# A fused attention and maxout kernel: columns of h by chunks of two batches, one store for a tile of 128 rows

## The chip, the cores and the metric

The kernel runs on one core of one Trainium2 chip. The core has a matrix engine (TensorE, PE in the profile, with its weight loads as PEld), a vector engine (VectorE, DVE), a scalar engine (ScalarE, ACT), GpSimd (POOL) and a synchronising engine (SyncE, SP). SP, ScalarE and GpSimd can issue transfers, which 16 DMA engines carry out. The metric is the device time in microseconds of one execution. Unless it says otherwise, a time inside an execution counts from the start of the profiled span.

## The reference, cut to what matters

Attention over 8 batches, 12 heads, 448 positions and 64 dimensions a head; its output, 3584 rows of 768, goes through three weight matrices, an elementwise maximum of the three products, and a fourth matrix.

```python
scores = scale * np.matmul(q, k.transpose(0, 1, 3, 2))
m = np.max(scores, axis=-1, keepdims=True)
e = np.exp(scores - m)
attn = e / (np.sum(e, axis=-1, keepdims=True) + np.exp(-m) + 1e-09)
attn_out = np.matmul(attn, v)                                # (8, 12, 448, 64)
x = attn_out.transpose(0, 2, 1, 3).reshape(B * S, H * D)     # (3584, 768)
h = np.maximum(np.maximum(x @ w1, x @ w2), x @ w3)
out = h @ w_out                                              # (3584, 768), float32
```

## The kernel before

**Tiles.** Everything is kept transposed: xT and hT have the 768 columns on the partitions (6 blocks of 128) and the positions along the free axis. A position s of a batch is split as s = 7p + j, with p from 0 to 63 and j from 0 to 6; the kernel's column for it is j * 64 + p, so a batch has 7 chunks (j) of 64 columns. Two batches share one hT tile of 6 x 896 columns, 448 of the first batch and then 448 of the second. The last product takes 128 columns of hT at a time as its stationary operand and gives an output tile of 128 rows by 768 columns; a pair of batches has 7 such tiles (t = 0 to 6). Rows 0 to 63 of a tile are one chunk and rows 64 to 127 the next, which at t = 3 belong to different batches. As the rows of a chunk lie 7 rows apart in the output, `store` (L582) sends each tile in two transfers of 64 rows.

**Order.** Attention runs by groups of four heads and feeds the products ("pieces") of finished batches into TensorE's free time, by a planner with costs (`book`, `first_free`, `step`). Pairs 0 and 1 (batches 0 to 3) are wholly done that way: `up_piece` (L507) makes h, `out_piece` (L554) makes the output. For batches 4 and 5 `up_piece` makes only a part of the blocks of h. The rest of pair 2 (batches 4 and 5) and all of pair 3 (batches 6 and 7) is done after the attention by `late_pair` (L1052), with Strassen-like products of 2 x 2 blocks: seven products in place of eight. Their order is written out by hand at the end (L1278 to L1314).

- `up_unit(i, f)` makes 2 x 128 rows of x @ w_i for both batches. `product` (L1035) accumulates three matmuls in a PSUM bank; `copy` (L1106) lets ScalarE evict a product that another one needs; `put` (L1091) evicts a sum into h (i = 0) or into the tile c, by VectorE with an addition (L1097) or by ScalarE alone (L1095). `largest` (L1104) takes the maximum of h and c over all columns. In the last pair the third weight's maxima are taken piece by piece (L1100, L1139).
- `h_sum` (L1083) makes the sums of blocks of h that the last product needs; a block is 3 x 384 columns.
- `out_unit(m)` makes the output tiles t = m (named o1) and t = 3 + m (o2) in column halves of 384 (`put`, L1157). VectorE adds two terms (L1168). The half of o1 that needs no second term goes through ScalarE (L1162), but through VectorE (L1164) where `late` holds, which is so in the last pair for m = 1 and 2.
- `last_tile` makes t = 6 by a plain product (L1232), evicted by VectorE (L1212) into o_last.

**Stores.** In pairs 0 to 2 both transfers of a tile are issued by SP. In the last pair the tile's column halves are sent as they come (except o2 for m = 1 and 2, which go whole); the first 64 rows are issued by SP and the other 64 by GpSimd, or by ScalarE for m = 2 and for o_last. A queue issues in order: an issue that waits for its data holds those behind it. The transfers of SP and ScalarE take eight completion semaphores in turn, and an issue waits until the transfer that had its semaphore before has landed.

Of the kernel before, what the change touches and what calls it, by code (L numbers as in the profile page):

```python
# [12 lines left out]
AF = mybir.ActivationFunctionType  # L13
ALU = mybir.AluOpType
ts = bass.ts

MMDT = FP16
LAMBDA = 256.0
# [4 lines left out]
def kernel(  # L23
# [11 lines left out]
    nc = tc.nc  # L35

    B, H, S, D = q.shape
# [66 lines left out]
    def half(n):  # L104
        return slice(n * KC, n * KC + KC)
# [394 lines left out]
    hT = {}  # L500
    outs = {}

    def new_h(b, fc, i):
        if b // 2 not in hT:
            hT[b // 2] = ht_pool.tile([128, NFC, 2 * S], MMDT, tag="hT", name="hT")

    def up_piece(b, fc, i, bank=None, done=False):  # L507
        if not done:
            new_h(b, fc, i)
        dst = hT[b // 2][:, fc, (b % 2) * S : (b % 2) * S + S]  # L510
        p_i = single("p_i") if bank is None else bank
        for dc in range(0 if done else NDC):
            nc.tensor.matmul(
                out=p_i[:, 0:S],
                lhsT=w_sb[i][:, dc, ts(fc, 128)],
                rhs=xT[b][:, dc, :],
                start=(dc == 0),
                stop=(dc == NDC - 1),
            )
        if i == 0 and done and first_free(2.8, 2.25) == "act":  # L520
            nc.scalar.activation(out=dst, in_=p_i[:, 0:S], func=AF.Copy)
        elif i == 0:
            nc.vector.tensor_copy(out=dst, in_=p_i[:, 0:S])
        else:
            book("dve", 2.8, steps[0] + 2)
            nc.vector.tensor_tensor(out=dst, in0=dst, in1=p_i[:, 0:S], op=ALU.max)  # L526

    def up_part(b, fp, i, part, bank=None):
        if fp == 0 and i == 0 and part == 0:
# [49 lines left out]
        if nh == NH - 1:  # L579
            store(2 * bp, t, o_sb, slice(0, DM))  # L580

    def store(b0, t, src, cols, engines=(nc.sync, nc.sync)):  # L582
        for n in range(2):
            b, j = divmod(2 * t + n, NJ)
            rows = out[(b0 + b) * S : (b0 + b + 1) * S].rearrange("(p j) m -> j p m", j=NJ)
            engines[n].dma_start(out=rows[j][:, cols], in_=src[half(n)])  # L586

    pieces = []

# [35 lines left out]
            run_job()  # L625

    NI = len(groups)
    PE_TR = 8

    load_weight(0, 0, 256)  # L630
# [265 lines left out]

    LATE = B - 4
    BESIDE = (0, 1)  # L900
    SOONER = 1

# [149 lines left out]
    def late_pair(p):  # L1052
# [32 lines left out]
        def up_unit(i, f):  # L1085
            w, t = w_sb[i], comb[i]
            u = {}
            c0 = slice(f * 128, f * 128 + 128)
            c1 = slice(DFF // 2 + f * 128, DFF // 2 + f * 128 + 128)

            def put(b, side, bank, other=None):  # L1091
                dst = hp if i == 0 else u["c"]
                dst = dst[:, f + 3 * side if i == 0 else side, b * S : b * S + S]
                if other is None:
                    nc.scalar.activation(out=dst, in_=bank, func=AF.Copy)  # L1095
                else:
                    nc.vector.tensor_tensor(out=dst, in0=other, in1=bank, op=ALU.add)  # L1097
                if i == 2 and ending:
                    h = hp[:, f + 3 * side, b * S : b * S + S]
                    nc.vector.tensor_tensor(out=h, in0=h, in1=dst, op=ALU.max)  # L1100

            def largest():
                dst = hp[:, f:NFC:3]
                nc.vector.tensor_tensor(out=dst, in0=dst, in1=u["c"], op=ALU.max)  # L1104

            def copy(name, bank):  # L1106
                u[name] = part(name, S)
                nc.scalar.activation(out=u[name], in_=bank, func=AF.Copy)

            def p1():  # L1110
                bank_of(u, "a")
                copy("p1", product(u, "a", lambda k: w[:, k, c0], lambda k: x1[:, k], S, True))

            def p2():
                bank_of(u, "s")
                bank = product(u, "s", lambda k: w[:, 3 + k, c0], lambda k: x1[:, 3 + k], S, True)
                if i > 0:
                    u["c"] = tail.tile([128, 2, 2 * S], MMDT, tag="c", name="c", bufs=3)
                put(0, 0, bank, u["p1"])

            def p6():
                copy("u2", product(u, "a", lambda k: t[:, 1, k, c0], lambda k: sx[p, 1][:, k], S, False))

            def p7():
                copy("p7", product(u, "s", lambda k: t[:, 2, k, c0], lambda k: sx[p, 2][:, k], S, True))

            def p5():
                bank = product(u, "a", lambda k: t[:, 0, k, c0], lambda k: sx[p, 0][:, k], S, False)
                put(1, 1, bank, u["p7"])

            def p4():
                bank = product(u, "s", lambda k: t[:, 3, k, c0], lambda k: x2[:, 3 + k], S, False)
                put(1, 0, bank, u["u2"])

            def p3():
                bank = product(u, "a", lambda k: w[:, 3 + k, c1], lambda k: sx[p, 3][:, k], S, False)
                if i == 2 and ending:
                    dst = hp[:, f + 3, 0:S]
                    nc.vector.tensor_tensor(out=dst, in0=dst, in1=bank, op=ALU.max)  # L1139
                else:  # L1140
                    put(0, 1, bank)

            if i == 0:
                return [p1, p2, p7, p6, p5, p4, p3]
            return [p1, p2, p6, p7, p5, p4, p3, largest]

        def out_unit(m):
            t = comb[3]
            u = {}
            r0 = slice(m * 128, m * 128 + 128)  # L1150
            r1 = slice(NT3 + m * 128, NT3 + m * 128 + 128)

            def copy(name, bank):
                u[name] = part(name, S)[:, 0:NW]
                nc.scalar.activation(out=u[name], in_=bank, func=AF.Copy, scale=1.0 / LAMBDA)

            def put(o, nh, bank, other=None, late=m == 2 and ending):  # L1157

                engines = nc.sync, nc.scalar if late else nc.gpsimd
                dst = u[o][:, ts(nh, NW)]  # L1160
                if other is None and not late:
                    nc.scalar.activation(out=dst, in_=bank, func=AF.Copy, scale=1.0 / LAMBDA)  # L1162
                elif other is None:
                    nc.vector.tensor_scalar(  # L1164
                        out=dst, in0=bank, scalar1=1.0 / LAMBDA, scalar2=None, op0=ALU.mult
                    )
                else:
                    nc.vector.scalar_tensor_tensor(  # L1168
                        out=dst, in0=bank, scalar=1.0 / LAMBDA, in1=other, op0=ALU.mult, op1=ALU.add
                    )  # L1170
                t = {"o1": m, "o2": 3 + m}[o]
                if ending and (o == "o1" or m == 0):
                    store(b0, t, dst, ts(nh, NW), engines)
                elif nh == (1 if o == "o1" else 0):
                    store(b0, t, u[o], slice(0, DM), engines if ending else (nc.sync, nc.sync))

            def p1():
                bank_of(u, "a")
                copy("p1", product(u, "a", lambda k: hp[:, k, r0], lambda k: wout_sb[:, k, 0:NW], NW, True))

            def p2():
                bank_of(u, "s")
                u["o1"] = tail.tile([128, DM], FP32, tag="o1", name="o1", bufs=5)
                bank = product(u, "s", lambda k: hp[:, 3 + k, r0], lambda k: wout_sb[:, 3 + k, 0:NW], NW, True)
                put("o1", 0, bank, u["p1"], False)

            def p6():
                copy("u2", product(u, "a", lambda k: sh[1][:, k, r0], lambda k: t[:, 1, k], NW, False))

            def p7():  # L1190
                copy("p7", product(u, "s", lambda k: sh[2][:, k, r0], lambda k: t[:, 2, k], NW, True))

            def p5():
                u["o2"] = tail.tile([128, DM], FP32, tag="o2", name="o2", bufs=3)
                put("o2", 1, product(u, "a", lambda k: sh[0][:, k, r0], lambda k: t[:, 0, k], NW, False), u["p7"])

            def p4():
                put("o2", 0, product(u, "s", lambda k: hp[:, 3 + k, r1], lambda k: t[:, 3, k], NW, False), u["u2"])

            def p3():  # L1200
                bank = product(u, "a", lambda k: sh[3][:, k, r0], lambda k: wout_sb[:, 3 + k, NW:DM], NW, False)
                put("o1", 1, bank, late=ending and m > 0)

            return [p1, p2, p6, p7, p5, p4, p3]

        def last_tile():
# [3 lines left out]
            def columns(c0, c1, cuts, end=None):  # L1210
                def done(bank):
# [5 lines left out]
                        op0=ALU.mult,  # L1217
                    )
                    if end is not None:
                        store(b0, NT - 1, o_last[:, end], end, (nc.sync, nc.scalar if ending else nc.sync))  # L1220

                return plain(hp, NT - 1, c0, c1, cuts, done)

# [121 lines left out]
```

## Time and profile before

| | |
|---|---|
| median of 3 timed runs | 317.21 us (316.23 to 318.7) |
| the profiled execution | 315.63 us, its span 313.9 us |
| TensorE busy | 300.7 us, 96% |
| VectorE busy | 247.7 us, 79% |
| ScalarE busy | 230.7 us, 73% |
| GpSimd busy | 83.0 us, 26% |
| TensorE clock granted | 0.999 |
| bytes written to HBM | 11.01 MB |

The span runs from the program's first instruction to its last; the profiled execution's own time is longer than its span by what lies around it. Busy shares are means over stages with different limits: the attention fills the span up to about 235 us, the late pairs the rest. The profile's views used below are the page (engines, slices, chain), busy time by stretches (with the DMA engines' share and GB/s in its last columns), timelines of one engine or queue, groups of instructions by line and form (count, busy us, mean ns of one, idle time before them), and the list of transfers issued in a stretch (size, median us from issue to landing). In a timeline the columns are start, duration, engine, line, operation, out<-in, form and count; SPq and ACTq are the issuing queues of SP and ScalarE.

### The profile page before, as it was taken

To read this page: it belongs to the slowest core of one execution; us is meant where nothing else is said; L and a number is where in the kernel's file an instruction comes from. 1 tells how busy PE (TensorE), PEld (TensorE's weight loads), DVE (VectorE), ACT (ScalarE), POOL (GpSimd) and SP (SyncE) were. 2 spreads that over 40 slices of the span, in tenths; PEclk is the share of its full clock that TensorE was granted. 3 is DMA by queue.
4 is the path that set the end of the run, shared out by engine and by line. 5 is a ranking of instruction groups with operands and counts; after the bars stand their busy time and mean duration, and the time that the engine had idled before them with its cause. 6 is when DMAs were issued, how large, how long until landed. Compare 5 with 4: busy or idle time off the path is not lost.

```text
span 313.9 us, 11772 instructions
## 1 busy us (share of the span) xinstructions
PE 300.7 (96%) x5132; PEld 213.2 (68%) x5132; DVE 247.7 (79%) x456; ACT 230.7 (73%) x315; POOL 83.0 (26%) x137
## 2 busy tenths in 40 slices
PE   7779999999999999999999999999999999999992
PEld 5557777658999778777666767777765555556551
DVE  3667598999889788888887898877857994989753
ACT  1999859987888988889888899999845457451540
POOL 8644441220434333434332434010000000000220
PEclk9999999999999999999999999999999999999999
DMA  8999999699778999889999999950004000002687
GB/s 152 196 203 205 208 207 203 102 158 176 95 118 138 188 210 143 99 127 180 204 150 145 100 194 217 143 90 2 4 2 102 1 2 0 0 2 70 179 241 215
DMA packets 59348, 40.58 MB, mean 129 GB/s; under 512 B 32256, under 2 KB 56288, under 8 KB 59296
## 3 DMA queue, kind: packets, MB, share of 16 engines
q0 software_dynamic: 25104, 21.80, 47.8%
q1 hardware_dynamic: 33648, 17.21, 26.6%
q8 instruction: 40, 0.66, 0.8%
q10 hardware_dynamic: 544, 0.82, 0.8%
q14 instruction: 12, 0.10, 0.1%
HBM read 42.47 MB, written 11.01 MB: 170 GB/s over the span
## 4 chain that ended last, share of the span: by engine, by line
PE 85%; ACT 6%; DVE 3%; issue 2%; DMA 1%; DVEq 0%; ACTq 0%
PE piece L786 35%; PE bank_a L1038 11%; PE stp L297 9%; PE bank_s L1038 8%; PE av L345 8%; PE p_i L537 4%; ACT eTp L419 3%; PE bank_a L1240 2%; PE piece L537 2%; ACT eT L321 2%; PE den L345 2%; DMA first_k<-in_k_dram 1%; PE piece L560 1%; DVE eS L331 1%; PE num L345 1%
## 5 line engine op out<-in xcount | busy, mean ns | idle before, releaser
L321 ACT ACTIVATE eT<-stp 128x896 f16<-128x896 f32 x147 | 128.9, 920 | 20.5 <-PE stp L297 20.4
L786 PE MATMUL piece<-xT,w 64*64 64x448 f16 x1968 | 120.6, 349 | 0.4 <-DVE xT L400 0.3
L786 PEld LDWEIGHTS <-w 64*64 64x64 f16 x1968 | 76.8, 107 | 18.1 <-issue 1.1
L331 DVE TENSOR_TENSOR eS<-eS,eT 128x896 f16<-128x896 f16 x105 | 64.9, 618 | 3.4 <-ACT eT L321 0.2
L297 PE MATMUL stp<-qkT 64*64 64x448 f16 (+2 forms) x756 | 63.4, 334 | 3.0 <-issue 0.9
L526 DVE TENSOR_TENSOR hT<-hT,piece 128x448 f16<-128x448 f16 x52 | 32.2, 619 | 13.1 <-PE piece L786 8.1
L297 PEld LDWEIGHTS <-qkT 64*64 64x64 f16 x756 | 28.6, 105 | 17.4 <-issue 6.8
L345 PE MATMUL av<-eT,ld_v 64*64 64x448 f16 x588 | 32.2, 349 | 0.0
L400 DVE TENSOR_TENSOR xT<-av,rb 128x448 f16<-128x448 f32 x42 | 24.2, 618 | 8.3 <-PE av L345 6.9
L345 PEld LDWEIGHTS <-ld_v 64*64 64x64 f16 x756 | 26.1, 107 | 6.5 <-issue 0.5
L114 POOL DMA_DIRECT2D ld_v<-in_v_dram x28 | 16.8, 600 | 51.5 <-PE stp L297 31.7
L786 PE MATMUL piece<-w,hT 64*64 64x384 f16 x456 | 29.3, 323 | 0.1
L586 POOL DMA_DIRECT2D out_dram<-o x7 | 3.8, 538 | 93.7 <-DVE o L1168 92.1
L114 POOL DMA_DIRECT2D ld_k<-in_k_dram x26 | 15.4, 596 | 39.1 <-PE stp L297 34.7
L365 ACT ACTIVATE rb<-den 128x896 f32<-128x896 f32 x21 | 19.3, 917 | 8.2 <-PE den L345 8.1
L419 ACT ACTIVATE eTp<-stp 128x768 f16<-128x768 f32 (+3 forms) x24 | 18.1, 821 | 6.0 <-PE stp L297 5.9
L537 PEld LDWEIGHTS <-w 128*128 128x128 f16 x216 | 18.7, 98 | 5.0 <-issue 3.5
L1038 PEld LDWEIGHTS <-comb 128*128 128x128 f16 x132 | 12.9, 98 | 12.2 <-issue 0.4
L786 PEld LDWEIGHTS <-hT 64*64 64x64 f16 x456 | 18.5, 107 | 3.7 <-issue 0.3
L372 ACT ACTIVATE rb<-rb 128x896 f32<-128x896 f32 x21 | 20.0, 952 | 0.2
L537 PE MATMUL p_i<-xT,w 128*128 128x192 f16 (+1 forms) x156 | 16.5, 257 | 0.0
L114 POOL DMA_DIRECT2D ld_q<-in_q_dram x26 | 15.7, 616 | 1.1 <-issue 1.1
(103 smaller groups left out, 404.9 us busy)
## 6 DMA issues: line engine op xcount, KB each, us to landing
out_dram<-o_sb SPq DMA_DIRECT2D x28, 192.0 KB, 4.6
ld_v<-in_v_dram POOLq DMA_DIRECT2D x28, 112.0 KB, 4.1
ld_k<-in_k_dram POOLq DMA_DIRECT2D x26, 112.0 KB, 3.0
ld_q<-in_q_dram POOLq DMA_DIRECT2D x26, 112.0 KB, 4.0
out_dram<-o SPq DMA_DIRECT2D x14, 192.0 KB, 3.1
ld_q<-in_q_dram POOLq DMA_DIRECT2D x11, 224.0 KB, 9.2
ld_k<-in_k_dram POOLq DMA_DIRECT2D x10, 224.0 KB, 9.3
ld_v<-in_v_dram POOLq DMA_DIRECT2D x10, 224.0 KB, 8.5
```

The costliest lines, as they stand in the source:

```text
L114: return eng.dma_start(out=dst[half(hp)].rearrange("p s j d -> p s (j d)"), in_=rows_of(name, i)[half(hp)])
L297: mm = nc.tensor.matmul(out=out[half(c), r], lhsT=qkT[half(r), 0, j, h], rhs=qkT[half(r), 1, q0:q1, h], start=True, stop=True,)
L321: nc.scalar.activation(out=st["eT"][:, j], in_=stp[:, :, 0:S], func=AF.Exp, scale=scale, bias=-math.log(EDIV))
L331: nc.vector.tensor_tensor(out=st["eS"], in0=st["eT"][:, 0] if j == 1 else st["eS"], in1=st["eT"][:, j], op=ALU.add,)
L345: nc.tensor.matmul(out=outs[r][half(c)], lhsT=weights(r, c), rhs=moving(r, c), start=start, stop=stop,)
L372: nc.scalar.activation(out=st["rb"], in_=st["rb"], func=AF.Exp, bias=math.log(LAMBDA), scale=-1.0)
L400: nc.vector.tensor_tensor(out=xT[b][:, 2 * g + r, :], in0=banks[r][:, 0:S], in1=state[i]["rb"][:, r], op=ALU.mult)
L419: nc.scalar.activation(out=eT[:, j0 : j0 + n].rearrange("p j r q -> p r j q"), in_=stp[:, :, 0 : n * nq].rearrange("p r (j q) -> p r j q", ...
L526: nc.vector.tensor_tensor(out=dst, in0=dst, in1=p_i[:, 0:S], op=ALU.max)
L537: nc.tensor.matmul(out=p_i[:, ts(j, nq)], lhsT=w_sb[i][:, dc, ts(2 * fp + j, 128)], rhs=xT[b][:, dc, q0 * KC : q1 * KC], start=(dc == 0), ...
L786: nc.tensor.matmul(out=p["bank"][half(c), 0:w], lhsT=lhs(k, r, c), rhs=rhs(k, r), start=(r == p["first"] and k == 0), stop=(r != p["first" ...
L1038: nc.tensor.matmul(out=bank, lhsT=lhs(k), rhs=rhs(k), start=start and k == 0, stop=k == 2, skip_group_check=True,)
```

## The change

For batches 4 to 7 the columns of h (and of the tile c) are ordered by chunk first and by batch second: column j * 128 + n * 64 + p for batch n of the pair. So an eviction of one batch's 448 columns writes 7 runs of 64 columns, 128 apart (`h_columns`), and reads its bank in the same shape (`by_chunk`). An output tile then holds chunk t of both batches; with 448 = 64 * 7 its 128 rows lie 7 rows apart throughout, across the batches' border, and one transfer stores them.

The stores of the last pair are all issued by SP, except the second column half of t = 2, which ScalarE issues. The second output of m = 2 (t = 5) is sent in two column halves. The second column halves of t = 1 and t = 2 of the last pair are evicted by ScalarE in place of VectorE. The tile o_last stays with VectorE.

Against the program before, the order of the computing instructions on each engine is the same but for those two evictions; VectorE has two instructions fewer and ScalarE two more. ScalarE's instructions in the late pairs gain 19 waits for VectorE, and TensorE one wait for an earlier matmul of its own.

```diff
+    def h_columns(t, b):
+        if b < LATE:
+            return t[:, (b % 2) * S : (b % 2) * S + S].rearrange("p (j q) -> p j q", j=NJ)
+        return t.rearrange("p (j n q) -> p n j q", j=NJ, n=2)[:, b % 2]
+
+    def by_chunk(t):
+        return t.rearrange("p (j q) -> p j q", j=NJ)
...
-        dst = hT[b // 2][:, fc, (b % 2) * S : (b % 2) * S + S]
+        dst = h_columns(hT[b // 2][:, fc], b)
...
-    def store(b0, t, src, cols, engines=(nc.sync, nc.sync)):
+    def store(b0, t, src, cols, engine=nc.sync):
+        if b0 >= LATE:
+            rows = out[b0 * S : (b0 + 2) * S].rearrange("(p j) m -> j p m", j=NJ)
+            engine.dma_start(out=rows[t][:, cols], in_=src)
+            return
         for n in range(2):
             b, j = divmod(2 * t + n, NJ)
             rows = out[(b0 + b) * S : (b0 + b + 1) * S].rearrange("(p j) m -> j p m", j=NJ)
-            engines[n].dma_start(out=rows[j][:, cols], in_=src[half(n)])
+            engine.dma_start(out=rows[j][:, cols], in_=src[half(n)])
...
             def put(b, side, bank, other=None):
-                dst = hp if i == 0 else u["c"]
-                dst = dst[:, f + 3 * side if i == 0 else side, b * S : b * S + S]
+                dst = h_columns((hp if i == 0 else u["c"])[:, f + 3 * side if i == 0 else side], b0 + b)
                 if other is None:
-                    nc.scalar.activation(out=dst, in_=bank, func=AF.Copy)
+                    nc.scalar.activation(out=dst, in_=by_chunk(bank), func=AF.Copy)
                 else:
-                    nc.vector.tensor_tensor(out=dst, in0=other, in1=bank, op=ALU.add)
+                    nc.vector.tensor_tensor(out=dst, in0=by_chunk(other), in1=by_chunk(bank), op=ALU.add)
                 if i == 2 and ending:
-                    h = hp[:, f + 3 * side, b * S : b * S + S]
+                    h = h_columns(hp[:, f + 3 * side], b0 + b)
                     nc.vector.tensor_tensor(out=h, in0=h, in1=dst, op=ALU.max)
...
-            def put(o, nh, bank, other=None, late=m == 2 and ending):
-
-                engines = nc.sync, nc.scalar if late else nc.gpsimd
+            def put(o, nh, bank, other=None):
                 dst = u[o][:, ts(nh, NW)]
-                if other is None and not late:
+                if other is None:
                     nc.scalar.activation(out=dst, in_=bank, func=AF.Copy, scale=1.0 / LAMBDA)
-                elif other is None:
-                    nc.vector.tensor_scalar(
-                        out=dst, in0=bank, scalar1=1.0 / LAMBDA, scalar2=None, op0=ALU.mult
-                    )
                 else:
...
-                if ending and (o == "o1" or m == 0):
-                    store(b0, t, dst, ts(nh, NW), engines)
+                if ending and (o == "o1" or m != 1):
+                    store(b0, t, dst, ts(nh, NW), nc.scalar if t == 2 and nh == 1 else nc.sync)
                 elif nh == (1 if o == "o1" else 0):
-                    store(b0, t, u[o], slice(0, DM), engines if ending else (nc.sync, nc.sync))
+                    store(b0, t, u[o], slice(0, DM))
...
-                        store(b0, NT - 1, o_last[:, end], end, (nc.sync, nc.scalar if ending else nc.sync))
+                        store(b0, NT - 1, o_last[:, end], end)
```

More of the change, by code (lines that the diff above doesn't have):

```diff
@@ L520, in up_piece @@
         if i == 0 and done and first_free(2.8, 2.25) == "act":
-            nc.scalar.activation(out=dst, in_=p_i[:, 0:S], func=AF.Copy)
+            nc.scalar.activation(out=dst, in_=by_chunk(p_i[:, 0:S]), func=AF.Copy)
         elif i == 0:
-            nc.vector.tensor_copy(out=dst, in_=p_i[:, 0:S])
+            nc.vector.tensor_copy(out=dst, in_=by_chunk(p_i[:, 0:S]))
         else:
             book("dve", 2.8, steps[0] + 2)
-            nc.vector.tensor_tensor(out=dst, in0=dst, in1=p_i[:, 0:S], op=ALU.max)
+            nc.vector.tensor_tensor(out=dst, in0=dst, in1=by_chunk(p_i[:, 0:S]), op=ALU.max)
     def up_part(b, fp, i, part, bank=None):
@@ L627 @@
     NI = len(groups)
+    LATE = B - 4
     PE_TR = 8
@@ L894 @@
     TOTAL = sum(w for _, _, w in ORDER)
-    LATE = B - 4
     BESIDE = (0, 1)
@@ L1137, in p3 @@
                 if i == 2 and ending:
-                    dst = hp[:, f + 3, 0:S]
-                    nc.vector.tensor_tensor(out=dst, in0=dst, in1=bank, op=ALU.max)
+                    dst = h_columns(hp[:, f + 3], b0)
+                    nc.vector.tensor_tensor(out=dst, in0=dst, in1=by_chunk(bank), op=ALU.max)
                 else:
@@ L1184, in p2 @@
                 bank = product(u, "s", lambda k: hp[:, 3 + k, r0], lambda k: wout_sb[:, 3 + k, 0:NW], NW, True)
-                put("o1", 0, bank, u["p1"], False)
+                put("o1", 0, bank, u["p1"])
             def p6():
@@ L1201, in p3 @@
                 bank = product(u, "a", lambda k: sh[3][:, k, r0], lambda k: wout_sb[:, 3 + k, NW:DM], NW, False)
-                put("o1", 1, bank, late=ending and m > 0)
+                put("o1", 1, bank)
             return [p1, p2, p6, p7, p5, p4, p3]
```

## The prediction

> **What bounds the kernel now.** I read the page first (engines, DMA slices), then the last 30 us by stretches, then the timelines of SP's queue and of VectorE, and last the DMA issues with their time to landing.
>
> ```profile
> span 313.9 us, 11772 instructions
> ...
> PE 300.7 (96%) x5132; PEld 213.2 (68%) x5132; DVE 247.7 (79%) x456; ACT 230.7 (73%) x315; POOL 83.0 (26%) x137
> ...
> DMA  8999999699778999889999999950004000002687
> ...
> PE 85%; ACT 6%; DVE 3%; issue 2%; DMA 1%; DVEq 0%; ACTq 0%
> ```
>
> TensorE is busy 96% of the span and makes 85% of the chain. So almost nothing the change does off TensorE can show before the last matmul. But the DMA digits end in 2687: in the last tenth of the span the engines that move data fill up again, and the chain of the page stops at the last computing instruction, so what the stores cost behind it is not in it. That is where I look.
>
> ```profile
> core 0: us, PE busy (x) PEld busy (x) DVE busy (x) ACT busy (x) POOL busy (x), PEclk, DMA share, GB/s
> ...
> 288.10:288.90 0.80, 0.80 (x8) 0.54 (x7) 0.38 (x1) 0.49 (x1) 0.00 (x0) 1.00 0.99 211
> 289.00:289.30 0.30, 0.30 (x7) 0.30 (x5) 0.30 (x1) 0.00 (x0) 0.00 (x0) 1.00 0.85 328
> 302.50:304.50 2.00, 2.00 (x14) 1.21 (x13) 1.11 (x2) 1.21 (x3) 0.08 (x1) 1.00 0.93 238
> ...
> 306.50:308.50 2.00, 1.65 (x17) 1.22 (x14) 1.98 (x5) 0.00 (x0) 0.00 (x0) 1.00 0.90 260
> 308.50:310.50 2.00, 0.00 (x0) 0.00 (x0) 0.05 (x1) 0.00 (x0) 0.00 (x0) 1.00 0.91 267
> 310.50:312.00 1.50, 0.00 (x0) 0.00 (x0) 0.00 (x0) 0.00 (x0) 0.00 (x0) 1.00 0.92 304
> ```
>
> The last column is GB/s, the one before it the busy share of the 16 DMA engines. From 302.5 us to 312.0 us that share never falls under 0.90, so the stores are a queue of their own by then, though they move only 238 to 304 GB/s. The first row holds one transfer of 64 rows alone: busy 0.99 and yet 211 GB/s. In the second the next half has joined, some engines have run ahead, and 328 GB/s pass. All arithmetic ends near 308.5 us, and 5.3 us of the span follow.
>
> ```profile
> 306.98 0.84 SPq L586 DMA_DIRECT2D out_dram<-o_last  x1
> 307.91 1.58 SPq L586 DMA_DIRECT2D out_dram<-o  x2
> 309.68 0.80 SPq L586 DMA_DIRECT2D out_dram<-o_last  x1
> ```
>
> ```profile
> 307.69 0.56 DVE L1164 TENSOR_SCALAR o<-bank_a 128x384 f32<-128x384 f32 x1
> 308.19 0.36 DVE L1212 TENSOR_SCALAR o_last<-bank_a 128x192 f32<-128x192 f32 x1
> ```
>
> ```profile
> out_dram<-o_last SPq DMA_DIRECT2D x1, 96.0 KB, 3.1
> ```
>
> The last eviction ends at 308.19 + 0.36 = 308.55 us. SP issues its store only at 309.68: two earlier issues stand before it, and it then waits for the semaphore that ScalarE's store of o_last (issued 306.32) frees by landing at 309.62. It lands 3.1 us later, at 312.75, and the closing instructions take 1.1 us to 313.86.
>
> **The change, part by part.** The profiled execution took 315.63 us, span 313.86 and 1.77 around it, 1.6 us under the median of 317.21 of the three timed runs. I make the sum in the span and take it off the median.
>
> *1. One transfer of 128 rows in place of two of 64 (batches 4 to 7).* In the stretch of the output tiles, from 286.9 us, SP issues 26 stores, POOL 7 and ScalarE 5, 38 in all for 14 tiles of 384 KB. After it SP issues 19 and ScalarE 1, with the same bytes; tile 5 now goes in two column halves. POOL's 7 issues were on no chain and give nothing. The price of a 128-row transfer is not in this trace. For its time to land, the nearest rows are these:
>
> ```profile
> out_dram<-o SPq DMA_DIRECT2D x2, 192.0 KB, 2.7
> ```
>
> ```profile
> out_dram<-o SPq DMA_DIRECT2D x1, 96.0 KB, 2.2
> ```
>
> Both met idle DMA engines (issued 286.94 and 295.41). The last store of the changed kernel is 192 KB in 128 rows: not under 2.2 us, and not over 2.7 if no backlog is left. I take 2.4, since at 328 GB/s its 197 kB move in 0.6 us and not in the 0.9 of the 211 GB/s row.
>
> Is the backlog gone by then? From 302.5 to 308.5 us the stores now move about 2 x (238 + 290 + 260) = 1.58 MB (the middle stretch moved 290). At 328 GB/s the same 6 us hold 1.97 MB, 0.39 MB more. After 308.5 us 267 x 2 + 304 x 1.5 = 0.99 MB are still moved, of which 0.39 MB are the two pieces that are evicted last. So of 0.60 MB of backlog 0.2 MB are left by this price, 0.6 us of traffic, most of it gone before the last store's first packet (1.1 us behind its issue in the 286.94 one). I add 0.2 us. Ends: 0 and 0.6.
>
> [...]
>
> *2. SP's queue.* With one transfer for two, the issues ahead of the last store are those of o_last's first half (ready at 306.29), and of tile 5's two halves (306.95 and 307.42). An issue takes SP 0.47 us with nothing behind it (rows from 286.94 on, 64 rows, whatever their width). So SP stands free at about 308.0, and issues the last store at 308.57 instead of 309.68. The semaphore that it then waits for belongs to the eighth DMA before it, the store of tile 1's second half, which was evicted at 302.43 and has long landed. Bounds for an issue of 128 rows: 0.47, and twice that, 0.94, where SP is late (a rival below). I take 0.5, the row of one DMA instruction of the same kind.
>
> *3. Evictions moved to ScalarE.* The words of the change say "last tile"; in the diff it is the second column half of tiles 1 and 2 of the last pair that move from VectorE (two of L1164, 0.55 us) to ScalarE (L1162, 0.49). The tile called o_last stays on VectorE. ScalarE is 0.5 us and less busy in each of the last stretches, and loses five DMA issues of about 0.5 us; its store of tile 2 stands behind its own eviction, at the end of its queue. The last eviction waits for TensorE, whose last matmul ends at 308.15, not for VectorE: gain 0 to 0.05 us, I take 0. If ScalarE were late, only tile 2's store would be: 0.5 us of slack towards the last one.
>
> *4. Columns of h by chunks.* All evictions of h and c for batches 4 to 7 write 7 runs of 64 instead of 448 in a row; matmuls read the same 128 columns in a row. Nearest rows:
>
> ```profile
> L214 DVE COPY qk<-ld_k 128x896 f16<-128x896 f16 x16 | 6.4, 402 | 0.0
> ...
> L257 DVE COPY qkT<-trT 128x896 f16<-128x896 f16 x8 | 4.6, 614 | 0.0
> L239 DVE COPY qkT<-trT 128x896 f16<-128x896 f16 x6 | 3.6, 620 | 0.9 <-PE trT L223 0.9
> L1100 DVE TENSOR_TENSOR hT<-hT,c 128x448 f16<-128x448 f16 x9 | 3.5, 392 | 0.3
> ```
>
> L257 writes runs of 64 from PSUM in 614 ns, L239 the same size in one run in 620; L214 works in runs of 64 on both sides at 402 ns for 896. So runs of 64 cost nothing on a copy. A two-operand instruction in SBUF with such runs (L1100) is not shown: between 392 ns and the 618 of the PSUM form of the same size. I take 392, as its rate is what L214 keeps or beats. ScalarE's evictions of h (544 ns) I leave as they are; half of its last stage is idle and covers 0.1 us each.
>
> *5. Waits.* The order of instructions on TensorE, VectorE and ScalarE is kept up to the last tiles. ScalarE gains 19 waits for VectorE, since the interleaved halves of a tile now overlap as ranges. In the trace the awaited instruction had ended 0.8 us or more before ScalarE's start in every one of them (closest: L1095 at 247.44, VectorE done at 246.62). Behind them stand ScalarE's next evictions and then TensorE's banks; while the 0.8 us hold, nothing moves. TensorE gets one wait for its own earlier matmul, at most 0.65 - 0.49 = 0.16 us, and SP's closing waits (28 ns each, some 60 ns apart) meet the last landing up to three earlier: together 0 to 0.35 us, I take 0.15.
>
> **Sum:** 308.57 + 2.4 + 0.2 = 311.17 for the landing (312.75 before), closing 1.1 + 0.15: a span of 312.4, 1.45 us less. With the ends: 308.57 + 2.2 + 1.1 = 311.9 (gain 2.0), and 308.57 + 2.7 + 0.6 + 1.45 = 313.3 (gain 0.55). Time: 317.21 - 1.45 = 315.8 us.
>
> **Rivals.**
>
> *The stores do not move faster.* If 64 rows are not what holds them, but the memory they go to, the rates stay at 260 to 300 GB/s, the last bytes still pass at 312.2, and the gain is 0 to 0.3: 317.1 us. For it: 3072-byte packets of both halves together never kept 328 for longer than fractions of a microsecond. Against it: 211 GB/s with one half alone and all 16 engines busy.
>
> *SP becomes the bound.* If an issue of 128 rows takes 0.94 us, the three issues from 306.29 end at 309.1, the last starts then, and the gain shrinks by 0.55: 316.4 us. For it: all but one store now stand in one queue. Against it: SP has 19 issues in 22 us in place of 26. [...]
>
> *Slower: the runs of 64 slow VectorE.* From 270 to 288 us VectorE is what TensorE waits for (2.4 us of the chain at 275.2 to 277.7 are ScalarE and VectorE; VectorE is busy 9.33 of 10 us from 280). There 21 of its instructions (9 L1097, 9 L1100, 3 L1139) get runs of 64. At 69 ns more each, passed on whole, my 1.45 us are spent. If L1100 alone falls to 618 ns, 9 x 0.226 = 2.0 us: 317.8 us. If all 21 lose it, 4.7 us: 320.5 us. Against it: L257, L239, L214.
>
> **How the numbers follow.** Forecast (gain 0.9 to 2.0) 0.65; stores no faster 0.14; SP the bound 0.12; VectorE slower 0.09, a third of that in the dear form. Three timed runs lie from 1.0 under to 1.5 over their median, so a median itself may be off by half a microsecond or more. The range starts at 315.2 (gain 2.0) less 1.4 of scatter, 313.8, and reaches to the cheap form of the slow rival, 317.8. About 1%, 3.2 us, is what a measurement of this kernel can tell from no change: the largest gain of the sum, 2.0, stays under it. Faster by over 1%: 0.08, by scatter or by something I do not see; slower by over 1%: 0.03, the dear form; within: 0.89.
>
> **What would show it.** Right: single out_dram issues of 192 KB and 384 KB on SP, none on POOL; a busy share under 0.8 with 300 GB/s and more from 303 us; last SP issue within 0.1 us of the last o_last eviction, landing 2.2 to 2.8 us later; the last matmul again at about 308.15 us. Wrong: L1100 over 420 ns or L1097 over 640; issues of SP near 0.9 us; a last landing over 3 us; a wait of ScalarE for VectorE in L1095 that moves TensorE's next bank.

## The result and the profile after

The changed kernel takes 314.99 us (median of 22 runs, 313.97 to 319.35) where the kernel before, run beside it, takes 316.55 us (median of 22). The ratio is 0.9947, 95% interval 0.9927 to 0.9968: faster, by about half a per cent. Predicted were 1.45 us, from 317.21 to 315.8 us; the two medians lie 1.56 us apart. The profiled execution took 314.43 us, its span 312.6 us (before 315.63 and 313.9).

The page of the changed kernel, the lines that were shown of before:

```profile
span 312.6 us, 11752 instructions
...
PE 300.7 (96%) x5132; PEld 212.9 (68%) x5132; DVE 247.0 (79%) x454; ACT 231.5 (74%) x317; POOL 79.0 (25%) x130
...
DMA  8999999789778999989999799950003000001466
...
PE 84%; ACT 8%; DVE 3%; issue 2%; DMA 1%; DVEq 0%; ACTq 0%
```

TensorE is as busy as before. What differs are the last DMA digits, 1466 for 2687: the same bytes no longer fill the engines. The stretches of the end show it (columns as before: the last is GB/s, the one ahead of it the busy share of the DMA engines):

```profile
core 0: us, PE busy (x) PEld busy (x) DVE busy (x) ACT busy (x) POOL busy (x), PEclk, DMA share, GB/s
288.30:289.20 0.90, 0.90 (x9) 0.64 (x8) 0.41 (x2) 0.49 (x1) 0.00 (x0) 1.00 1.00 396
302.50:304.50 2.00, 2.00 (x15) 1.21 (x13) 1.10 (x2) 1.03 (x3) 0.00 (x0) 1.00 0.79 310
304.50:306.50 2.00, 2.00 (x14) 1.22 (x13) 0.54 (x1) 0.98 (x3) 0.00 (x0) 1.00 1.01 390
306.50:308.50 2.00, 1.88 (x18) 1.33 (x16) 1.38 (x5) 0.49 (x1) 0.00 (x0) 1.00 0.76 279
308.50:310.50 2.00, 0.00 (x0) 0.00 (x0) 0.28 (x1) 0.00 (x0) 0.00 (x0) 1.00 0.78 286
310.50:311.40 0.90, 0.00 (x0) 0.00 (x0) 0.00 (x0) 0.00 (x0) 0.00 (x0) 1.00 0.14 48
```

With the share at 1.00 and 1.01, 396 and 390 GB/s pass, where a busy share of 0.90 to 0.98 moved 238 to 304 before. In the stretches at 0.76 to 0.79 the engines are idle for a fifth of the time or more, as less is sent. The queue of SP, and the last rows of VectorE:

```profile
306.55 0.33 SPq L595 DMA_DIRECT2D out_dram<-o_last  x1
307.09 1.37 SPq L595 DMA_DIRECT2D out_dram<-o  x2
308.80 0.33 SPq L595 DMA_DIRECT2D out_dram<-o_last  x1
```

```profile
307.45 0.35 DVE L1219 TENSOR_SCALAR o_last<-bank_a 128x192 f32<-128x192 f32 x1
308.42 0.36 DVE L1219 TENSOR_SCALAR o_last<-bank_a 128x192 f32<-128x192 f32 x1 [0.62 <-PE bank_a L1247]
```

The last eviction ends at 308.78 and SP issues its store at 308.80, 0.02 us later; before it was 1.13. The list of issues from 308.6 us on gives the landing, and the DMA engines in slices of 0.11 us:

```profile
DMA  0005999999998999992000000000000000000000
GB/s 14 28 14 196 335 377 405 349 377 349 377 391 349 363 405 349 363 335 84 28 28 14 0 0 0 0 0 0 0 0 0 0 0 0 0 0 0 0 0 0
...
out_dram<-o ACTq DMA_DIRECT2D x1, 192.0 KB, 2.5
out_dram<-o_last SPq DMA_DIRECT2D x1, 192.0 KB, 2.6
```

The engines stand at nothing when the last two stores are issued (the first three digits): no backlog is left, and both pass at 335 to 405 GB/s. The last lands 2.56 us after its issue (3.07 before). Last, the operations with strided columns. They took 618 (the first line, of before), 392 and 544 ns before:

```profile
L1097 DVE TENSOR_TENSOR c<-p,bank_a 128x448 f16<-128x448 f32 x8 | 4.8, 618 | 3.7 <-ACT p L1108 3.7
```

```profile
L1110 DVE TENSOR_TENSOR c<-p,bank_a 128x448 f16<-128x448 f32 x8 | 4.8, 618 | 3.7 <-ACT p L1121 3.7
L1113 DVE TENSOR_TENSOR hT<-hT,c 128x448 f16<-128x448 f16 x9 | 3.5, 392 | 0.3
L1108 ACT ACTIVATE c<-bank_a 128x448 f16<-128x448 f32 x5 | 2.7, 543 | 5.9 <-PE bank_a L1052 5.7
```

One thing has to be taken out before executions are compared. The last matmul ends at 308.39 us here and at 308.15 before, and in the executions profiled below it ends anywhere from 308.5 to 312.6 us, with the same work for TensorE. The 0.24 us are there from the start of the span on (TensorE is busy 53.22 us of the first 60, and 53.45 before), and are no part of the change. So the measure for a profile is the time **from the end of the last eviction**, to the last landing and to the end of the span:

| profiled | last issue | last landing | end of the span | ratio to before (95%) |
|---|---|---|---|---|
| before | 1.13 | 4.20 | 5.31 | 1 |
| after | 0.02 | 2.58 | 3.86 | 0.9947 (0.9927 to 0.9968) |

The gain is 1.45 us there: 1.11 from the issue, 0.51 from the landing, and 0.17 given back by the closing instructions (1.28 us for 1.11).

### The profile page after: what moved, and what is told of

It reads as the page before. It is cut to its first block, busy times and chain, and to the rows that moved or that the text cites. A ratio compares the mean times of both kernels' runs of the same rounds, so it can differ in the third digit from the quotient of the medians.

```text
span 312.6 us, 11752 instructions
## 1 busy us (share of the span) xinstructions
PE 300.7 (96%) x5132; PEld 212.9 (68%) x5132; DVE 247.0 (79%) x454; ACT 231.5 (74%) x317; POOL 79.0 (25%) x130
## 4 chain that ended last, share of the span: by engine, by line
PE 84%; ACT 8%; DVE 3%; issue 2%; DMA 1%; DVEq 0%; ACTq 0%
PE piece L801 35%; PE bank_a L1052 11%; PE stp L297 9%; PE bank_s L1052 8%; PE av L345 8%; PE p_i L547 4%; ACT eTp L419 3%; PE bank_a L1247 3%; PE piece L547 2%; ACT eT L321 2%; PE den L345 2%; DMA first_k<-in_k_dram 1%; PE piece L570 1%; DVE eS L331 1%; ACT rb L463 1%
## 5 line engine op out<-in xcount | busy, mean ns | idle before, releaser
L547 PEld LDWEIGHTS <-w 128*128 128x128 f16 x216 | 18.7, 98 | 5.0 <-issue 3.5
L1052 PEld LDWEIGHTS <-w 128*128 128x128 f16 x99 | 9.7, 98 | 9.0 <-issue 0.2
```

The costliest lines, as they stand in the source:

```text
L547: nc.tensor.matmul(out=p_i[:, ts(j, nq)], lhsT=w_sb[i][:, dc, ts(2 * fp + j, 128)], rhs=xT[b][:, dc, q0 * KC : q1 * KC], start=(dc == 0), ...
L1052: nc.tensor.matmul(out=bank, lhsT=lhs(k), rhs=rhs(k), start=start and k == 0, stop=k == 2, skip_group_check=True,)
```

## The experiments

Theory T: what pays is that each transfer reads from the whole range of the partitions; halves of 64 neighbouring rows are moved slowly, fill the DMA engines in the last 10 us, and so delay landings, semaphores and the last store. The rivals: the column order and the two evictions on ScalarE pay (E); the smaller number of transfers and their places in the queues pay. All kernels are the changed one with the edit shown (later ones of a group against the first of it), each timed in five rounds against the kernel before (twelve runs of each, but four and six of the first two on SP alone).

**Where it comes from: four ways to store a tile on the queues of before.** The first kernel puts the stores back, and leaves column order and evictions as changed. `half(n)` is rows 0 to 63 or 64 to 127. Tile 5 goes whole again, as before.

```diff
-            engine.dma_start(out=rows[t][:, cols], in_=src)
+            other = engine if b0 < B - 2 else nc.scalar if t in (2, 5, NT - 1) else nc.gpsimd
+            for n in range(2):
+                (engine, other)[n].dma_start(out=rows[t][half(n), cols], in_=src[half(n)])
...
-                if ending and (o == "o1" or m != 1):
-                    store(b0, t, dst, ts(nh, NW), nc.scalar if t == 2 and nh == 1 else nc.sync)
+                if ending and (o == "o1" or m == 0):
+                    store(b0, t, dst, ts(nh, NW), nc.sync)
```

> The changed kernel with its stores of batches 4 to 7 cut again into rows 0 to 63 and rows 64 to 127, on the queues of before (SP, GpSimd, ScalarE); order of columns, evictions on ScalarE and all else as changed. Theory T (64 rows of one half of the partitions are what slows the stores): the tail returns, 240 to 300 GB/s from 303 us at a busy share near 0.9, last landing 4 us after the last eviction, ratio to before 0.998 to 1.002. Rival Q (what counts is the number of transfers and issues, 38 against 20): the same ratio, 1.000. Rival E (the evictions moved to ScalarE, or the order of columns, make the gain): 0.995 as in the changed kernel.

Measured: 1.0024 (0.9999 to 1.005), a little over T's 1.002. The gain is gone, so neither the column order nor the evictions carry it. Once more, on one chip with the two kernels that follow:

> The 64-row halves on three queues once more, on the same chip as the two beside it, so that the split between rate and number of transfers is read from one set of runs. T: ratio 1.000 to 1.004, last eviction to the end of the span 5.0 to 5.4 us. Rival (its first profile was an odd one, started 4 us late): under 4.5 us, ratio under 0.999.

Measured: 1.0012 (0.9977 to 1.0047). The second kernel has the same number of transfers of 64 rows on the same queues, but each takes every second row:

```diff
-                (engine, other)[n].dma_start(out=rows[t][half(n), cols], in_=src[half(n)])
+                (engine, other)[n].dma_start(out=rows[t][n::2, cols], in_=src[n::2])
```

> As e1 (38 transfers of 64 rows, the three queues of before), but each transfer takes every second partition. e2 and e3 were both held by SP's issues, so this is the pair that tells rate from count. T (one half of the partitions is what is slow): packets of 3072 bytes at some 123 ns as in e3 and not 180 as in e1, no backlog, last issue within 0.4 us of the last eviction, ratio 0.994 to 0.998. Q (number of transfers and issues): as e1, 1.000 to 1.004.

> Every second row in each of two transfers, the same three queues, beside the other two. T (rate pays nearly all): last eviction to the end of the span 3.9 to 4.3 us, ratio 0.993 to 0.998, that is 0.004 to 0.006 below the contiguous halves. Rival (the number of transfers pays at least half): ratio within 0.002 of the contiguous halves.

Measured: 0.9976 (0.9939 to 1.0012) and 0.9952 (0.9919 to 0.9985). The last issue comes 0.62 us after the last eviction and not within the 0.4 that were expected. The third has two transfers for each store again on these queues, of all 128 rows and half the columns each:

```diff
+            dst, w = rows[t][:, cols], src.shape[1] // 2
             for n in range(2):
-                (engine, other)[n].dma_start(out=rows[t][half(n), cols], in_=src[half(n)])
+                (engine, other)[n].dma_start(out=dst[:, n * w : n * w + w], in_=src[:, n * w : n * w + w])
```

> The queues and the 31 issues of the last pair and of the kernel before, but each transfer holds all 128 rows and half of the columns; nothing of partitions is halved. T (coverage of the partitions is what pays, at the end of the span): from the last eviction to the end of the span 3.8 to 4.2 us (5.2 with halves of 64 rows on the same queues, 3.85 with one transfer), ratio to the kernel before 0.993 to 0.998. Rival (the number of transfers and the queues they stand in pay): 4.8 to 5.3 us after the last eviction, ratio 1.000 to 1.004.

Measured: 0.9966 (0.993 to 1.0002). (The last pair has 24 transfers on these queues, 12 of SP, 7 of GpSimd and 5 of ScalarE; the 31 of the expectation is a miscount.) The intervals of these ratios overlap, as each also carries the spread of the kernel before. Side by side on one chip the median times are 317.06 us with neighbouring rows, 315.28 with every second row and 315.31 with halves of columns, and seven of the twelve runs with every second row lie below all twelve with neighbouring rows (315.70 and more). The profiles show where the difference arises. The last 6 us of work and what follows, for the halves of neighbouring rows (the second run), for every second row (the second run), and for the halves of columns:

```profile
303.00:309.00 6.00, 5.60 (x40) 3.48 (x37) 3.23 (x7) 1.82 (x5) 0.43 (x1) 1.00 0.93 261
309.00:312.80 3.80, 0.00 (x0) 0.00 (x0) 0.07 (x1) 0.04 (x1) 0.00 (x0) 1.00 0.82 257
```

```profile
304.00:310.00 6.00, 5.50 (x39) 3.44 (x37) 3.30 (x7) 1.76 (x5) 0.36 (x1) 1.00 0.74 281
310.00:312.50 2.50, 0.00 (x0) 0.00 (x0) 0.00 (x0) 0.00 (x0) 0.00 (x0) 0.81 0.84 317
```

```profile
304.00:310.00 6.00, 5.46 (x39) 3.39 (x37) 3.26 (x7) 1.85 (x4) 0.31 (x1) 1.00 0.81 287
310.00:312.20 2.20, 0.00 (x0) 0.00 (x0) 0.00 (x0) 0.00 (x0) 0.00 (x0) 1.00 0.72 234
```

Only the first is full while work goes on (0.93 at 261 GB/s), and leaves 257 x 3.8 = 0.98 MB for the time after; the others have 0.79 and 0.51 MB left. In the trace a packet of 3072 bytes takes 184 ns in the mean with neighbouring rows (from 303 to 313 us), and 124 ns with every second row, or 16.7 and 24.7 GB/s for an engine. The issues of ScalarE and SP that end the two kernels, and what they took to land (issues from 306 us on), first neighbouring rows, then every second:

```profile
out_dram<-o SPq DMA_DIRECT2D x3, 192.0 KB, 3.7
out_dram<-o_last ACTq DMA_DIRECT2D x2, 96.0 KB, 3.3
out_dram<-o_last SPq DMA_DIRECT2D x2, 96.0 KB, 3.2
```

```profile
out_dram<-o SPq DMA_DIRECT2D x3, 192.0 KB, 2.2
...
out_dram<-o_last ACTq DMA_DIRECT2D x2, 96.0 KB, 2.5
out_dram<-o_last SPq DMA_DIRECT2D x2, 96.0 KB, 2.3
```

From the end of the last eviction (runs of one kernel side by side):

| a store of the last pair | last issue | last landing | end of the span |
|---|---|---|---|
| 2 x 64 neighbouring rows, three queues | 1.06, 1.19 | 4.10, 4.00 | 5.19, 5.11 |
| 2 x every second row, three queues | 0.62, 0.62 | 2.85, 2.84 | 4.07, 4.05 |
| 2 x half the columns, three queues | 0.12 | 2.56 | 3.65 |
| after (one transfer) | 0.02 | 2.58 | 3.86 |

Every second row gives 1.06 to 1.12 us with nothing else changed: same number of transfers, rows, bytes and queues. That is some 85% of the way from there to the changed kernel. Two transfers of 128 rows come out where one does, so their number pays nothing by itself on three queues. What T says of neighbouring halves stands. The timed ratios set the neighbouring rows apart from the others (every second row is 0.0048 and 0.0060 below them in the two sets of runs), but they do not order the others among themselves.

One thing these runs do not separate: with every second row the rows that are written lie 14 apart in the output and not 7. What speaks for the partitions that are read is that the kernel before and the first kernel here write differently (two neighbouring chunks, mostly of one batch; the same chunk of two batches) from the same halves of the partitions, and both are slow: 171 and 184 ns for a packet of 3072 bytes from 303 to 313 us. That the partitions are the cause and not the addresses written is so far argued, not shown.

**The number of issues, on SP alone.** Three kernels send two transfers for each store on the queue that the changed kernel uses. First halves of neighbouring rows, then every second row:

```diff
-            engine.dma_start(out=rows[t][:, cols], in_=src)
+            for n in range(2):
+                engine.dma_start(out=rows[t][half(n), cols], in_=src[half(n)])
```

> As e1, but all halves issued by SP (ScalarE issues the two of tile 2's last half). T: rates as in e1, and one queue in place of three: ratio 1.000 to 1.005. Q: SP alone now has 38 issues of 0.35 to 0.6 us in 22 us and waits for eight semaphores: 1.003 to 1.010. E: 0.995.

Measured: 1.0126 (1.0101 to 1.0151), above the ranges of T and of its rival alike.

```diff
-                engine.dma_start(out=rows[t][half(n), cols], in_=src[half(n)])
+                engine.dma_start(out=rows[t][n::2, cols], in_=src[n::2])
```

> As e2, with as many transfers of 64 rows, but each takes every second partition (0, 2, 4 ... and 1, 3, 5 ...) in place of one half. T: each transfer reaches all of the partitions' range, so 350 GB/s and more, no backlog at the end, ratio 0.994 to 0.998, last landing under 3 us. Q: the same as e2, 1.003 to 1.010. If 64 rows as such are slow, whichever they are: rates as in e2.

Measured: 1.0123 (1.009 to 1.0156), far from T's ratio. A packet of 3072 bytes did take 123 ns (194 with neighbouring rows, both from 303 to 313 us), and the engines were not full, 0.58 in the 6 us up to 309. But SP could not keep up; its queue in the kernel with every second row:

```profile
304.44 4.45 SPq L596 DMA_DIRECT2D out_dram<-o  x7
308.99 2.34 SPq L596 DMA_DIRECT2D out_dram<-o_last  x2
311.42 2.46 SPq L596 DMA_DIRECT2D out_dram<-o  x4
313.98 1.18 SPq L596 DMA_DIRECT2D out_dram<-o_last  x2
```

An issue of 64 rows takes SP 0.47 us with nothing ahead of it and 0.54 to 0.6 behind another. The row at 308.99 holds a wait besides: of SP's waits in this stretch the longest is

```profile
SPq L596 <- DMA out_dram<-o: 1.3, 1, 1.3
```

The second transfer of o_last's first half takes the semaphore that ScalarE's store of tile 2 (issued at 308.56, behind its own late eviction) still holds; SP stands from 309.54 until that store lands at 310.83, and then issues this one and six more in turn. The last is issued 5.7 us after the last eviction. With neighbouring rows the same wait lasts till 312.03. T's ratio left out both, while the rival named them (1.003 to 1.010) and sized them too low; as a test of the rate by its ratio the kernel says nothing, which is why every second row was tried on three queues. Third, halves of the columns, against the changed kernel:

```diff
-            engine.dma_start(out=rows[t][:, cols], in_=src)
+            dst, m = rows[t][:, cols], src.shape[1] // 2
+            for n in range(2):
+                engine.dma_start(out=dst[:, n * m : n * m + m], in_=src[:, n * m : n * m + m])
```

> As many transfers as e2, but each of all 128 rows and half the columns. T: 350 GB/s and more, less what pieces of 768 and 1536 bytes lose; ratio 0.994 to 0.998. Q: as e2, 1.003 to 1.010. E: 0.995.

Measured: 0.9969 (0.9948 to 0.999). An issue of 128 rows takes 0.33 to 0.46 us here (one of them 0.77), so SP falls behind by less: its last issue comes 1.4 us after the last eviction, the landing 3.13 and the end of the span 4.18 us after it. Nearly the gain of the changed kernel remains with twice the transfers on one queue.

**The two evictions back on VectorE:**

```diff
-                if other is None:
+                if other is None and not (ending and m > 0):
                     nc.scalar.activation(out=dst, in_=bank, func=AF.Copy, scale=1.0 / LAMBDA)
+                elif other is None:
+                    nc.vector.tensor_scalar(
+                        out=dst, in0=bank, scalar1=1.0 / LAMBDA, scalar2=None, op0=ALU.mult
+                    )
```

> The changed kernel with the two evictions given back to VectorE. T: nothing depends on them, 0.994 to 0.996 as in the changed kernel. E (the move to ScalarE carries part of the gain): 0.996 to 1.000.

Measured: 0.9941 (0.9907 to 0.9976), the last issue 0.03, the landing 2.39 and the end of the span 3.67 us after the last eviction. Nothing is lost without this part of the change.

**All stores on SP,** tile 2's last half too:

```diff
-                    store(b0, t, dst, ts(nh, NW), nc.scalar if t == 2 and nh == 1 else nc.sync)
+                    store(b0, t, dst, ts(nh, NW), nc.sync)
```

> The changed kernel with tile 2's last store on SP too, ahead of the very last one. T with a price of 0.33 us for an issue of 128 rows: SP issues it at 308.45 and the last one at 308.8, the same end, 0.994 to 0.996. If issues of SP are what is short (Q): the last one 0.3 to 0.9 us later, 0.996 to 0.998.

Measured: 0.9967 (0.9933 to 1.0001). SP issues tile 2's half at 309.39 and o_last's at 309.82, 0.09 us behind its eviction; it lands 2.74 and the span ends 4.02 us after that eviction. The ratio lies in the range of the rival (0.996 to 0.998), but its interval takes in the changed kernel's too, and the last issue is not the 0.3 to 0.9 us later that the rival asks for. So SP is no bound with one transfer for a store; whether ScalarE's single issue is worth 0.1 us or nothing, these intervals cannot tell.

**A smaller last store.** The last half of o_last in two pieces of 192 columns, each sent when it is evicted:

```diff
-                + columns(NW, NW + NW // 2, ())
-                + columns(NW + NW // 2, DM, (), slice(NW if ending else 0, DM))
+                + columns(NW, NW + NW // 2, (), slice(NW, NW + NW // 2) if ending else None)
+                + columns(NW + NW // 2, DM, (), slice(NW + NW // 2 if ending else 0, DM))
```

> The changed kernel with the last column half of o_last stored in two pieces of 192 columns, each when it is evicted. T: the landing of the last piece falls from 2.56 us to 1.7 to 2.2 us behind its issue (98 KB), and ScalarE's store of tile 2 (2.46 us) becomes the last to land: 0.3 to 0.5 us less, ratio 0.992 to 0.995. If a landing costs the same whatever its size: no change, 0.9947.

Measured: 0.9954 (0.9925 to 0.9983), no gain over the changed kernel, where 0.992 to 0.995 were expected; SP's queue at the end:

```profile
308.29 0.33 SPq L595 DMA_DIRECT2D out_dram<-o_last  x1
308.84 1.31 SPq L595 DMA_DIRECT2D out_dram<-o  x2
310.25 0.89 SPq L595 DMA_DIRECT2D out_dram<-o_last  x2
```

The second issue of tile 5 takes 0.85 us and ends at 310.15, so the first piece, ready at 309.54, is issued at 310.25 and the last at 310.72, 0.20 us behind its eviction. It lands after 2.38 us in place of 2.56 (1.7 to 2.2 were expected), and both end 2.58 us after the last eviction. No version tried is clearly under the changed kernel.

## Why the prediction was right, step by step

The place, the mechanism and the sum held; single terms were off in ways that cancelled or lay beside other work.

- **Step 1, one transfer for two.** Right, and the cause of the gain: every second row alone gives 1.06 to 1.12 us, three quarters of the 1.45, and halves of columns give all of it with as many transfers as before. The rate was sized too low: 328 GB/s assumed, 390 to 396 measured at a share of 1.00. So the 0.2 us of backlog that I added are not there (the engines stand idle at 308.6 us). The landing took 2.56 us and not 2.4. ScalarE's store, issued 0.36 us ahead, is under way beside it, but that this is why is not shown: the same store took 2.37 and 2.66 us in two other kernels, and one of half its size 2.38. With 2.6 us for both terms the sum was right, for half of a wrong reason and so in part by luck. The pair of kernels with 64 rows in each transfer shows that it matters which rows those are (184 ns for a packet of 3072 bytes with neighbouring rows, 124 with every second row). Both halves of neighbouring rows under way together do move more than one alone: 211 GB/s for one half (before, 288.1 to 288.9 us), and 258 and 261 with both (the two runs of the halves on three queues, shares of 0.90 and 0.93), 22% to 24% more.
- **Step 2, SP's queue.** The last issue follows the last eviction by 0.02 us (as predicted: 308.57 after 308.55). My price for an issue of 128 rows was 0.5 us; with SP idle ahead of it, it took 0.33. One issue, tile 5's second, took 0.91, which the prediction had named as a sign of being wrong; it ended 0.3 us before the last one was ready and cost nothing. That the issue of before was late for a semaphore was read correctly, but it is no second cause beside step 1: with halves of neighbouring rows on three queues the last issue is late by 1.06 and 1.19 us again (in the second run SP waits until 309.27 for the landing of its own store of 305.87, and its next issue takes 0.83 us); with every second row it is late by 0.62, as one issue of tile 2, 0.47 us on SP and 0.50 on ScalarE, stands ahead of it and begins only when ScalarE's eviction ends.
- **Step 3, evictions on ScalarE.** Worth nothing that shows, as said; undone, the ratio is 0.9941 (0.9907 to 0.9976).
- **Step 4, strided columns.** L1113 (L1100 before) takes 392 ns in both kernels, L1110 613 to 622 (L1097 before 612 to 621), ScalarE's eviction 543 (544).
- **Step 5, waits.** None of ScalarE's 19 new waits shows among what engines waited for. The closing instructions take 0.17 us more (0.15 taken).

**The rivals.** That the stores move no faster is excluded by 390 GB/s at a full share. That SP becomes the bound is excluded for the changed kernel, but it is what decides once a store is two transfers on SP: 1.0123 and 1.0126 are this rival, made real. That runs of 64 slow VectorE is excluded by its durations (392 ns in both kernels, and 613 to 622 for 612 to 621). Two of my signs of being right were not met as written. The last matmul was to end again at 308.15 us and missed by 0.24, since such a mark wanders from one execution to the next. And the busy share was to stay under 0.8 with 300 GB/s and more from 303 us on: it was 0.79 at 310 GB/s, then 1.01 at 390, then 0.76 at 279.

**What stays open.** The remaining 0.2 us between every second row and one transfer: in these profiles the last issue comes 0.6 us later and what it sends lands 0.35 us sooner, but there are one or two profiles for each kernel. Then whether the partitions read or the addresses written make the difference between the two kinds of 64 rows, as said above; why single issues of SP take 0.7 to 1.26 us in most profiles (tile 5's second 0.91, 0.85 and 0.70 in three) where the next of the same kind takes 0.33; and whether the closing instructions are longer by cause or by chance (1.0 to 1.3 us over the profiles).

## What to carry to other kernels

Where a busy share of the DMA engines near 1 goes with fewer GB/s than another stretch of the same kernel (before: 0.99 at 211, and 0.85 at 328), with packets of the same size, the transfers may be slow and not too many, as they were here: look at which rows each of them holds. A packet of 3072 bytes took 171 to 194 ns with 64 neighbouring rows in a transfer, and 123 to 124 with every second row or all 128. What ends after the last computing instruction is not on the chain of the page: read it from the last eviction to the last issue, to the last landing, to the end of the span, and compare executions by that, since the work ahead of it ended up to 4 us later in one execution than in another, which is more than such a gain. Putting the stores on one queue cost nothing here with one transfer for each (19 issues of SP in the last 22 us of work, the last of them 0.02 us behind its eviction); with two of every second row the last issue came 5.7 us behind it, 1.3 us of that a wait for a semaphore that ScalarE's store held. So count the issues against the time that is left, with the semaphores that they share with other queues.

## What the runs showed of the hardware that was not expected

- A transfer of 128 rows cost SP less to issue than one of 64: 0.33 us for 0.47 with nothing ahead of it, 0.39 to 0.46 for 0.54 to 0.6 behind another, apart from the single long issues named above.
- Two transfers of 64 rows that interleave row by row ran at the rate of one transfer of 128 rows (123 to 124 ns for a packet of 3072 bytes, and 124); two that split the rows in the middle did not (171 to 194 ns in the mean from 303 to 313 us), even while both were under way.
- The completion semaphores tied queues together: one late store of ScalarE held SP's queue for 1.3 us, with six more issues behind the one that waited, though neither needed the other's data.
